# Block products for two more token tiles, and the scan's later units packed closer

## The chip, the core and the metric

The kernel runs on one core of a Trainium2 chip. Its engines each work through their own instructions in program order and wait for one another by semaphores: TensorE (PE, with its weight loads as PEld), VectorE (DVE), ScalarE (ACT), GpSimd (POOL) and SyncE (SP), which here issues DMA transfers only. The metric is device time in microseconds of one execution. The kernel before takes 340.98 us (median of 3 runs, 340.87 to 345.75).

## The reference

A gated linear-attention scan over 4 batches, 8 heads and 768 positions, in chunks, is followed by a feed-forward layer over the 3072 tokens:

```python
# per chunk: cum = cumsum(log a); L = exp(cum_i - cum_j), causal
M = (C @ B^T) * L
y = M @ x + (C @ state) * exp(cum)
state = exp(sum(log a)) * state + sum_j B_j x_j exp(cum_end - cum_j)
# then, with x = y as 3072 x 256:
h = x @ w_in            # 256 -> 2048
g = maximum(0.01 * h, h)
out = g @ w_out         # 2048 -> 256
```

Results are kept to about float32: every float32 operand of the feed-forward matmuls is split into a high and a low part, and a product is three matmuls (high x high, low x high, high x low).

## The kernel before

**The scan.** Its chunk here is 96 positions (`Q`), so there are 8 chunks of 4 batches: 32 units. A unit makes scores on PE (128-partition score banks `sc`), multiplies them on DVE with a decay tile `lt`, and then makes its outputs and the next state on PE (`unit_products`). `unit_halves` copies the state out on ACT (`stage`), from which POOL writes four small copies into the next chunk's `xs`; ACT also copies the unit's outputs, 96 tokens, into the token tiles that the feed-forward layer reads, and for most tiles DVE makes the low part `xl` right there.

Units 0 to 5 come first by themselves. Units 6 to 15 go one to each of the feed-forward steps 0 to 9 (`UNIT`), with decay made by PE. Units 16 to 31 go by pairs (`PAIR`): their decay rows are broadcast from DRAM by SP (`decay_rows`), POOL subtracts a column (`decay_sub`, L264), ACT takes the exponential and POOL selects the causal part (`decay_exp`, L272 and L273). `pair_block` (L367) makes the outputs of the last pair, the scores of the new one, the four score products on DVE (L388) and the copies. A pair stands at every fourth step from 24 to 52, and `LAST_OUT`, 56, makes the last outputs.

**The feed-forward layer.** The 3072 tokens are six tiles of 512, and the 2048 hidden features are 16 blocks of 128. A step (`ffn_in`, `ffn_act`, `ffn_low`, `ffn_out`) handles one tile and one block: six matmuls into `hp`, two activations on ACT (high part `gh`, and the activation in place), the low part `gl` on DVE, and, three steps later (`LAG`), six matmuls into two accumulator banks `op`. `CELLS` lists which tile goes with which blocks in what order: tiles 0, 1 and 2 through blocks 0 to 4, then through 5 to 15, then tile 3 through all, 64 steps. Where a cell ends, both accumulators are read out (L528 adds to an earlier part on DVE; L532 on ACT and L534 on DVE copy), before the next cell may use the banks.

Weights arrive during the first steps, 16 blocks of 512 KB. Each is decoded from 64-bit floats by ACT and by five DVE passes; `decode(n)` issues n of them at the end of a step, and `PASSES` holds n for each step.

**Tiles 4 and 5** are done last, in `two_tiles`, by Winograd's form of Strassen's algorithm for the first layer: for two blocks and two tiles it makes seven products of three matmuls where eight are usual. That takes sums of weight blocks (`sums`, `sums_split`: POOL and ACT) and sums of the two tiles (`combine`: casts and subtractions, nearly all on DVE, with two subtractions on POOL), and sums of the products out of the banks on DVE (L780, L789, L790, L796, L797). There are eight groups. In each, `slot()` gives PE output matmuls of the group before as filler. For these tiles the scan writes float32 (`x32`) and no low part. `combine` is a generator; from step `COMBINE`, 57, one piece is issued at each step.

The order of every engine is the order of the program text (`manual_schedule`); in the main loop (L818 on) a step issues: the scan's due work (`early`), `ffn_in`, `ffn_act`, `ffn_low`, a pair block if due, decode passes, a piece of `combine`, then `late` work, and last the output matmuls of step s - 3 with a cell's read-out.

Of the kernel before, what the change touches and what calls it, by code (L numbers as in the profile page):

```python
# [10 lines left out]
F32 = mybir.dt.float32  # L11
F32R = mybir.dt.float32r
# [6 lines left out]
Q = 96  # L19
NC = S // Q  # L20
QE = Q + N
# [15 lines left out]
CELLS = ((0, 0, 5), (1, 0, 5), (2, 0, 5), (0, 5, 16), (1, 5, 16), (2, 5, 16), (3, 0, 16))  # L37
TWO = (4, 5)
# [22 lines left out]
def scan_ffn(ctx: ExitStack, tc: tile.TileContext, a_l, bc_l, bn_l, x_l, w_l, out_l):  # L61
# [4 lines left out]
    px = ctx.enter_context(tc.tile_pool(name="px", bufs=4))  # L66
    pg = ctx.enter_context(tc.tile_pool(name="pg", bufs=LAG + 1))
    pob = ctx.enter_context(tc.tile_pool(name="pob", bufs=3))
# [4 lines left out]
    plt = scan.enter_context(tc.tile_pool(name="plt", bufs=4))  # L73
# [55 lines left out]
    upto_b = const.tile([Q, QE], BF16, name="upto_b")  # L129
    after = const.tile([Q, QE], F32, name="after")  # L130
    later = const.tile([Q, Q], BF16, name="later")
    less = const.tile([128, NH], BF16, name="less")
    dl = const.tile([128, SLOTS, QE], BF16, name="dl")
    dr = const.tile([128, SLOTS, NH, Q], BF16, name="dr")
    reach = [const.tile([Q, NH, Q], F32, name=f"reach{i}") for i in range(DIRECT)]
# [194 lines left out]
    def unit_halves(u, space, off=0):  # L330
# [5 lines left out]
        while i < Q:  # L336
            t, col = divmod(u * Q + i, TS)
            n = min(Q - i, TS - col)
            if col == 0 and t in TWO:
                x32[t] = mix.tile([128, 2, TS], F32, name="x32")  # L340
# [11 lines left out]
        for t, to, of in pieces:  # L352
            nc.scalar.copy((x32 if t in TWO else xh)[t][:, :, to], yp[:, :, of])
        def rest():
            for t, to, of in pieces:
                if t in TWO:
# [40 lines left out]

    w_half = [const.tile([128, NF, 2 * DM], F32R, name=n) for n in ("wh", "wl")]
# [235 lines left out]
    at(late, EARLY[-1] + 2, late_sums)  # L634
# [14 lines left out]
    def open_mix():  # L649
        nonlocal mix  # L650
        wts.close()
        mix = ctx.enter_context(tc.tile_pool(name="mix", bufs=2, side="right", reuse_waits="tile"))

    mix = bx = sp = su = None

    def open_two():
        nonlocal bx, sp, su
        scan.close()
        bx = ctx.enter_context(tc.tile_pool(name="bx", bufs=1, reuse_waits="tile"))
        sp = ctx.enter_context(tc.tile_pool(name="sp", bufs=2, reuse_waits="tile"))  # L660
# [4 lines left out]
    def sums(p):  # L665
        w32 = sp.tile([128, 2, DM], F32, name="w2")
# [17 lines left out]
    rhs = {}  # L684

    def combine():
        t1, t2 = TWO
        a, b = x32[t1], x32[t2]
        t12 = mix.tile([128, 2, TS], F32, name="t14")
        t34 = mix.tile([128, 2, TS], F32, name="t14")  # L690
        names = ("xh", "xl")
        ab = [[px.tile([128, 2, TS], F32R, name=n) for n in names] for _ in range(3)]
        ab.append([bx.tile([128, 2, TS], F32R, name=n) for n in names])
        for (h, _), x, ks in zip(ab, (a, b), (slice(0, 2), slice(1, 2))):
            nc.vector.tensor_copy(h[:, ks], x[:, ks])
        yield
# [6 lines left out]
        nc.gpsimd.tensor_tensor(  # L703
            out=ab[1][1][:, 1], in0=b[:, 1], in1=ab[1][0][:, 1], op=ALU.subtract
        )
# [7 lines left out]
        for n, (i, k) in {"11": (0, 0), "21": (0, 1), "22": (1, 1), "t1": (2, 0), "t2": (2, 1),  # L713
                          "t3": (3, 0), "t4": (3, 1)}.items():
            rhs[n] = [y[:, k] for y in ab[i]]

# [18 lines left out]
    def two_out(f, t, gh, gl, first, last):  # L735
        for m in range(2):
# [5 lines left out]
            if last:  # L742
                keep_out(t, m, outs[t][m], t == TWO[1] and m == 1)

# [7 lines left out]
    def two_tiles(queue):  # L752
        t1, t2 = TWO
        banks = score_tile()
        B, C = banks[:, 0], banks[:, 1]
        tops = score_tile()
        outs[t1] = [tops[:, m] for m in range(2)]

        def slot():
            if queue:  # L760
                queue.popleft()()

        for p in range(NP):
# [17 lines left out]
            if p + 1 < NP:  # L781
                sums(p + 1)
            slot()
            if p == 0:
                outs[t2] = [ps_o.tile([128, TS], F32, name="op") for _ in range(2)]
# [13 lines left out]
            if p + 1 < NP:  # L799
                sums_split(p + 1)  # L800
# [6 lines left out]
            order = ("11", "21", "22", "12") if p == NP - 1 else ("11", "22", "21", "12")  # L807
# [5 lines left out]
        while queue:  # L813
            slot()
# [3 lines left out]
    for s in range(total):  # L818
# [27 lines left out]
        if not passes and mix is None:  # L846
            open_mix()
        if s == COMBINE:
# [3 lines left out]
            combining = combine()  # L852
# [50 lines left out]
```

## Time and profile before

| | |
|---|---|
| median of 3 runs | 340.98 us (340.87 to 345.75) |
| profiled execution | 342.04 us, span of its instructions 340.3 us |
| PE busy | 323.8 us, 95% of the span |
| DVE, ACT, POOL busy | 201.8, 179.3, 126.1 us |
| granted TensorE clock, mean | 0.978 |
| data moved by DMA | 27.79 MB |

The profile is of one execution, and its instructions' rows give a start, an engine, the line in the kernel, the operation, and the tiles as output<-inputs. Where an engine sat idle before an instruction, brackets give how long and what ended the wait. "Groups" put together the instructions of one line and engine; "the window table" sums up busy time by engine in a stretch of the span; "the chain of waits" is followed back from the last instruction.

### The profile page before, as it was taken

The numbers are of one execution on the slowest core, as the hardware profiler recorded it, in microseconds if no ns is written. First come the engines' busy times: TensorE is split into PE (matmuls) and PEld (weight loads), VectorE is DVE, ScalarE is ACT, GpSimd is POOL, SyncE is SP. The second block draws the span as 40 slices with busy tenths as digits, with TensorE's granted clock in tenths as the row PEclk, the third lists the DMA queues.
The fourth block names the chain that finished last, engine by engine and source line by source line (L and its number), as shares of the span: only waits on it lengthen the run. The fifth ranks groups of instructions, "written<-read, shape, count | busy, mean of one in ns | idle before, by whom it ended". The sixth has DMA issues, their size and how long they took to land.

```text
span 340.3 us, 6355 instructions
## 1 busy us (share of the span) xinstructions
PE 323.8 (95%) x2410; PEld 247.7 (73%) x2412; DVE 201.8 (59%) x343; ACT 179.3 (53%) x350; POOL 126.1 (37%) x214
## 2 busy tenths in 40 slices
PE   8978899999898999999999999999999999999994
PEld 4545576778677787788888887878876787777873
DVE  5767877875787454344263243429757667556561
ACT  6555645755565654545545545343445456454551
POOL 3751413220010352733753644309224665436100
PEclk9996789999999999999999999999999999999999
DMA  7755462312783002172065121000001000000003
GB/s 223 214 190 187 153 214 65 121 57 74 219 258 113 2 1 80 64 206 93 13 174 158 44 85 64 0 2 0 0 0 64 0 0 0 2 2 0 2 0 123
DMA packets 10638, 27.79 MB, mean 82 GB/s; under 512 B 2448, under 2 KB 2544, under 8 KB 10608
## 3 DMA queue, kind: packets, MB, share of 16 engines
q1 hardware_dynamic: 9920, 24.80, 23.3%
q10 hardware_dynamic: 688, 2.59, 2.4%
q8 instruction: 19, 0.31, 0.4%
q14 instruction: 11, 0.09, 0.1%
HBM read 24.01 MB, written 3.24 MB: 80 GB/s over the span
## 4 chain that ended last, share of the span: by engine, by line
PE 81%; DVE 8%; DMA 4%; ACT 3%; issue 1%; SPq 0%; ACTq 0%
PE hp L496 26%; PE op L520 24%; PE sc L719 8%; PE sc L738 6%; PE op L738 4%; PE sc L315 3%; PE hp L719 3%; DMA raw<-w_l 2%; PE sc L298 2%; PE sc L379 2%; DMA bn<-bn_l 2%; DVE u L789 2%; DVE c L790 2%; PE sc L324 1%; PE sc L244 1%
## 5 line engine op out<-in xcount | busy, mean ns | idle before, releaser
L509 DVE TENSOR_TENSOR gl<-hp,gh 128x512 fp32r<-128x512 f32 x64 | 44.2, 691 | 79.0 <-ACT hp L506 78.0
L503 ACT ACTIVATE gh<-hp 128x512 fp32r<-128x512 f32 x64 | 38.1, 595 | 63.0 <-PE hp L496 63.0
L520 PE MATMUL op<-gh,wh 128*128 128x512 f32 x128 | 52.4, 410 | 4.0 <-DVE ob L534 2.7
L496 PE MATMUL hp<-xh,wh 128*128 128x512 f32 x128 | 52.5, 410 | 0.0
L496 PE MATMUL hp<-xh,wl 128*128 128x512 f32 x128 | 51.3, 401 | 0.0
L496 PE MATMUL hp<-xl,wh 128*128 128x512 f32 x128 | 51.1, 399 | 0.0
L351 POOL COPY xs<-stage 16x64 f32<-16x64 f32 x112 | 28.5, 255 | 60.8 <-ACT stage L348 56.5
L520 PE MATMUL op<-gh,wl 128*128 128x512 f32 x128 | 50.0, 391 | 0.0
L520 PE MATMUL op<-gl,wh 128*128 128x512 f32 x128 | 49.9, 390 | 0.0
L506 ACT ACTIVATE hp<-hp 128x512 f32<-128x512 f32 x64 | 38.0, 594 | 0.0
L520 PEld LDWEIGHTS op<-gh,wh 128*128 128x128 f32 x128 | 24.0, 188 | 12.3 <-DVE ob L534 3.5
L264 POOL TENSOR_TENSOR lt<-lt,ccol 112x768 f32<-112x768 f32 x16 | 23.5, 1471 | 23.9 <-DMA lt<-crow_d 23.3
L682 POOL TENSOR_TENSOR sl<-s,sh 128x512 fp32r<-128x512 f32 x8 | 10.4, 1295 | 56.4 <-ACT sh L681 56.4
L496 PEld LDWEIGHTS hp<-xh,wh 128*128 128x128 f32 x128 | 24.6, 192 | 7.8 <-issue 2.6
L496 PEld LDWEIGHTS hp<-xl,wh 128*128 128x128 f32 x128 | 24.9, 194 | 5.5
L496 PEld LDWEIGHTS hp<-xh,wl 128*128 128x128 f32 x128 | 24.8, 194 | 4.9
L520 PEld LDWEIGHTS op<-gl,wh 128*128 128x128 f32 x128 | 24.0, 188 | 5.2
L520 PEld LDWEIGHTS op<-gh,wl 128*128 128x128 f32 x128 | 24.1, 188 | 4.3
L273 POOL TENSOR_SCALAR_AFFINE_SELECT lt<-lt 96x768 f32<-96x768 f32 x16 | 14.0, 877 | 31.0 <-ACT lt L272 31.0
L750 DVE TENSOR_TENSOR gl<-c,gh 128x512 fp32r<-128x512 f32 x24 | 22.4, 938 | 4.8 <-PE op L738 3.1
L746 ACT ACTIVATE gh<-c 128x512 fp32r<-128x512 f32 x24 | 15.2, 632 | 18.1 <-DVE c L790 9.5
L272 ACT ACTIVATE lt<-lt 112x768 f32<-112x768 f32 x16 | 13.5, 846 | 17.4 <-POOL lt L264 17.4
(144 smaller groups left out, 604.0 us busy)
## 6 DMA issues: line engine op xcount, KB each, us to landing
raw<-w_l SPq DMA_DIRECT2D x13, 512.0 KB
lt<-crow_d SPq DMA_DIRECT2D x16, 336.0 KB
bc<-bc_l SPq DMA_DIRECT2D x7, 608.0 KB
out_l<-ob SPq DMA_DIRECT2D x12, 256.0 KB
xs<-x_l SPq DMA_DIRECT2D x7, 384.0 KB
bn<-bn_l SPq DMA_DIRECT2D x8, 231.0 KB
raw<-w_l ACTq DMA_DIRECT2D x3, 512.0 KB
bc<-bc_l ACTq DMA_DIRECT2D x1, 608.0 KB
```

Of the source, the lines that this page charges most:

```text
L264: nc.gpsimd.tensor_tensor(out=lts[u], in0=lts[u], in1=ccol[:, u * NH:(u + 1) * NH].unsqueeze(2).to_broadcast([QE, NH, Q]), op=ALU.subtract,)
L273: nc.gpsimd.affine_select(out=lt[:Q], in_=lt[:Q], pattern=[[0, NH], [1, Q]], compare_op=ALU.is_ge, fill=0.0, base=0, channel_multiplier=-1,)
L351: nc.gpsimd.tensor_copy(to[:, :, hh], stage[hh * D:hh * D + N])
L496: nc.tensor.matmul(hp, lhsT=w_half[half][:, f, k * 128:(k + 1) * 128], rhs=x[t][:, k, :], start=(n == 0), stop=(n == 5),)
L503: nc.scalar.activation(ghs[s], hp, AF.Prelu, alpha=0.01)
L506: nc.scalar.activation(hps[s], hps[s], AF.Prelu, alpha=0.01)
L509: nc.vector.tensor_tensor(out=gls[s], in0=hps.pop(s), in1=ghs[s], op=ALU.subtract)
L520: nc.tensor.matmul(op, lhsT=w_half[half][:, f, DM + m * 128:DM + (m + 1) * 128], rhs=x, start=(first and i == 0), stop=(last and i == 2),)
L719: nc.tensor.matmul(bank, lhsT=w[h], rhs=x[g], start=start and i == 0, stop=i == 2, skip_group_check=True,)
L738: nc.tensor.matmul(outs[t][m], lhsT=w_half[half][:, f, DM + m * 128:DM + (m + 1) * 128], rhs=x, start=first and i == 0, stop=last and i == 2,)
L746: nc.scalar.activation(gh, h, AF.Prelu, alpha=0.01)
L750: nc.vector.tensor_tensor(out=gl, in0=g, in1=gh, op=ALU.subtract)
```

## The change

The six cells now are tiles 0 and 1 alone, through blocks 0 to 4, 5 to 9 and 10 to 15: 32 steps. Tiles 2 to 5 get float32 from the scan, and `two_tiles` runs twice, for (2, 3) and then (4, 5): sixteen groups. The pairs of scan units stand at every second step from 12 to 26, `LAST_OUT` and `COMBINE` at 28; each unit's decay is asked for four steps ahead rather than five, and with the pairs so close a chunk's loads are issued three steps ahead of its first pair (`max(b - 12, b0 + 1)`). The late sums move from step 11 to 6. From step 10 on, `decode` gets three and two passes by turns.

The first `combine`, for tiles 2 and 3, is issued from step 28; what is left of it follows the loop. Its pieces are regrouped: the cast of tile `a` and the first two subtractions now are one piece. The second `combine`, for tiles 4 and 5, is issued inside the first `two_tiles`, a piece after each group. Between the two runs of `two_tiles` the queue of output matmuls goes on: the second's accumulators are opened by an entry of the queue. Pools change with this: `px` and `pob` have 2 buffers, a pool `pw` of 4 holds the float32 tiles, `plt` has 6 buffers, and some constants move to a pool that is closed with the scan.

```diff
-CELLS = ((0, 0, 5), (1, 0, 5), (2, 0, 5), (0, 5, 16), (1, 5, 16), (2, 5, 16), (3, 0, 16))
-TWO = (4, 5)
+CELLS = ((0, 0, 5), (1, 0, 5), (0, 5, 10), (1, 5, 10), (0, 10, 16), (1, 10, 16))
+TWOS = ((2, 3), (4, 5))
...
-PAIR = {16: 24, 18: 28, 20: 32, 22: 36, 24: 40, 26: 44, 28: 48, 30: 52}
-LAST_OUT = 56
-COMBINE = 57
-
-PASSES = (5, 5, 5, 3, 3, 3, 3, 2, 3, 3) + (3,) * 12
+PAIR = {16: 12, 18: 14, 20: 16, 22: 18, 24: 20, 26: 22, 28: 24, 30: 26}
+LAST_OUT = 28
+COMBINE = 28
+SUMS_AT = 6
+
+PASSES = (5, 5, 5, 3, 3, 3, 3, 2, 3, 3) + (3, 2) * 8
...
-            at(early, b - 5 + e, decay_rows, u + e)
+            at(early, b - 4 + e, decay_rows, u + e)
             at(early, b - 3 + e, decay_sub, u + e)
             at(early, b - 2 + e, decay_exp, u + e)
...
-    def combine():
...
-        for (h, _), x, ks in zip(ab, (a, b), (slice(0, 2), slice(1, 2))):
-            nc.vector.tensor_copy(h[:, ks], x[:, ks])
-        yield
+    def combine(pair, pools, temps, rhs):
...
+        nc.vector.tensor_copy(ab[0][0], a)
         nc.vector.tensor_tensor(out=t12[:, 0], in0=b[:, 0], in1=a[:, 0], op=ALU.subtract)
         nc.vector.tensor_tensor(out=t34[:, 0], in0=b[:, 1], in1=b[:, 0], op=ALU.subtract)
         nc.gpsimd.tensor_tensor(out=ab[0][1], in0=a, in1=ab[0][0], op=ALU.subtract)
         yield
         nc.vector.tensor_tensor(out=t12[:, 1], in0=b[:, 1], in1=t12[:, 0], op=ALU.subtract)
         nc.vector.tensor_tensor(out=t34[:, 1], in0=a[:, 1], in1=t12[:, 1], op=ALU.subtract)
...
+        nc.vector.tensor_copy(ab[1][0], b[:, 1])
+        nc.gpsimd.tensor_tensor(out=ab[1][1], in0=b[:, 1], in1=ab[1][0], op=ALU.subtract)
         yield
...
+    def two_tiles(queue, pair, rhs, after_group):
...
+        def opens():
+            open_outs(t1, t2)
+
+        queue.append(opens)
...
-        while queue:
-            slot()
+            after_group(p)
...
-    two_tiles(collections.deque(
-        [lambda s=s: ffn_out(s) for s in range(total - LAG, total)]
-    ))
+    for _ in combining:
+        pass
+    queue = collections.deque([lambda s=s: ffn_out(s) for s in range(total - LAG, total)])
+    temps = [pw.tile([128, 2, TS], F32, name="x32") for _ in range(2)]
+    combining = combine(TWOS[1], (px, by, px, by), temps, rhs_of[1])
+    two_tiles(queue, TWOS[0], rhs_of[0], lambda p: next(combining, None))
+    two_tiles(queue, TWOS[1], rhs_of[1], lambda p: None)
+    while queue:
+        queue.popleft()()
```

More of the change, by code (lines that the diff above doesn't have):

```diff
@@ L741, in two_out @@
                 )
-            if last:
-                keep_out(t, m, outs[t][m], t == TWO[1] and m == 1)
+        if last:
+            for m in range(2):
+                keep_out(t, m, outs[t][m], t == NT - 1 and m == 1)
     def act_split(h, gh, in_place):
@@ L780, in two_tiles @@
             nc.vector.tensor_tensor(out=u2, in0=B, in1=kept, op=ALU.add)
-            if p + 1 < NP:
-                sums(p + 1)
+            if p + 1 < NP or t2 < NT - 1:
+                sums((p + 1) % NP)
             slot()
-            if p == 0:
-                outs[t2] = [ps_o.tile([128, TS], F32, name="op") for _ in range(2)]
             product(A, False, a12, rhs["21"])
@@ L851, in scan_ffn @@
             sums_split(0)
-            combining = combine()
+            with_temps = [su.tile([128, 2, TS], F32, name=n) for n in ("t12", "t34")]
+            rhs_of = [{}, {}]
+            combining = combine(TWOS[0], (bx,) * 4, with_temps, rhs_of[0])
         if combining:
```

88 lines of the change are left out of this document (44 added, 44 removed).

## The prediction

> **What bounds the kernel now.** I read the page first, then the chain of waits, then three stretches of the window table, then the timeline around every gap of the matmul engine. The page says that one engine is the program:
>
> ```profile
> span 340.3 us, 6355 instructions
> ...
> PE 323.8 (95%) x2410; PEld 247.7 (73%) x2412; DVE 201.8 (59%) x343; ACT 179.3 (53%) x350; POOL 126.1 (37%) x214
> ...
> PE 81%; DVE 8%; DMA 4%; ACT 3%; issue 1%; SPq 0%; ACTq 0%
> ```
>
> PE is busy for 95% of the span and carries 81% of the chain that ended last. So an edit pays only where it takes matmuls away, and costs wherever PE is made to wait. Three prices of PE work follow, from the chain of waits around 150 us (start, length, work) and the window table (the stretch, its length, then busy time of PE, PEld, DVE, ACT, POOL, granted clock, DMA share, GB/s):
>
> ```profile
> 151.31 1.36 PE hp L496 x6
> 152.67 1.36 PE op L520 x6
> ```
>
> ```profile
> 148.43:161.44 13.01, 13.01 (x129) 10.56 (x128) 5.34 (x11) 6.67 (x15) 6.54 (x12) 1.00 0.52 161
> 293.55:304.23 10.68, 10.53 (x45) 8.36 (x45) 6.78 (x10) 5.87 (x10) 5.43 (x6) 1.00 0.00 2
> ```
>
> A step of twelve matmuls takes 1.36 + 1.36 = 2.72 us, 0.227 us a matmul. The first stretch is four steps and one pair of scan units: 13.01 - 4 x 2.72 = 2.13 us of PE for a pair. The second stretch is one group of seven block products, 45 matmuls in 10.68 us, where four plain steps (48 matmuls) would take 10.88.
>
> **The exchange itself.** Tiles 2 and 3 leave 32 steps and become eight groups. By count that is 8 x 3 = 24 matmuls fewer, 24 x 0.227 = 5.4 us. But a group does not run at the matmul rate: 45 x 0.227 = 10.2, so 0.46 us of it is a wait, and the timeline shows which:
>
> ```profile
> 282.15 0.69 DVE L790 TENSOR_TENSOR c<-sc,u 128x512 f32<-128x512 f32 x1
> ...
> 282.36 0.39 PE L738 MATMUL op<-gl,wh 128*128 128x512 f32 x1
> 282.90 0.50 PE L719 MATMUL sc<-xh,wh 128*128 128x512 f32 x1
> ```
>
> The bank sums on DVE end at 282.84 and the next product starts behind them; PE's last filler, issued at 282.36, had its 0.23 us by 282.6. The new groups have the same order, so I price them alike: 32 x 2.72 - 8 x 10.68 = 87.0 - 85.4 = **1.6 us saved**. The scan's matmuls are the same in number, so packing the pairs changes PE's work by nothing; it changes what the other engines must do in the time.
>
> **Cell boundaries.** Where a cell ends, the accumulators in `op` must be read out before the next cell's first output matmul. PE's gaps at such places, and DVE's order at the first of them:
>
> ```profile
> 87.60 0.50 PE L520 MATMUL op<-gh,wh 128*128 128x512 f32 x1 [1.09 <-DVE ob L534]
> 103.14 0.50 PE L520 MATMUL op<-gh,wh 128*128 128x512 f32 x1 [1.61 <-DVE ob L534]
> 207.99 0.47 PE L520 MATMUL op<-gh,wh 128*128 128x512 f32 x1 [0.54 <-DVE ob L528]
> ```
>
> ```profile
> 84.94 0.68 DVE L443 TENSOR_TENSOR wl<-w,wh 128x512 fp32r<-128x512 f32 x1
> ...
> 86.86 0.68 DVE L534 COPY ob<-op 128x512 f32<-128x512 f32 x1
> ```
>
> Together 1.09 + 1.61 + 0.54 = 3.2 us now. DVE works in program order: three decode passes (84.94 to 86.86, 1.92 us) stand ahead of the read-out, and PE waits for it. In the new order the boundaries fall behind steps 12, 17, 22 and 28. Rows for what is put in between:
>
> ```profile
> 146.15 0.86 PE sc L379 x16
> ...
> 223.74 0.80 PE sc L315 x32
> ```
>
> ```profile
> 147.08 1.95 DVE L388 TENSOR_TENSOR lt<-sc,lt 112x384 f32<-112x384 f32 x4
> ```
>
> Step 12 (first pair): DVE gets four score products more, PE 0.86 us of scores: 1.09 + 1.95 - 0.86 = 2.2. Step 17: the following step has a pair, whose 2.13 us of PE cover it: 0. Step 22: 1.09 + 1.95 - 2.13, and 0.68 more because both read-outs are now DVE additions, so the first three matmuls wait, not the last three: 1.6. Step 28 is worse: its three decode passes are gone, but `COMBINE` now stands at 28, and the first piece of `combine` is issued ahead of that step's read-outs. Its instructions ran once in this trace:
>
> ```profile
> 231.20 2.52 POOL L699 TENSOR_TENSOR xl<-x,xh 128x1024 fp32r<-128x1024 f32 x1 [0.63 <-DVE xh L695]
> ```
>
> ```profile
> 232.03 2.23 DVE L697 TENSOR_TENSOR t<-x,x 128x512 f32<-128x512 f32 x1
> 234.19 1.78 DVE L698 TENSOR_TENSOR t<-x 128x512 f32<-128x512 f32 x1
> ...
> 239.06 1.64 DVE L708 CAST xh<-t 128x1024 fp32r<-128x1024 f32 x2
> 241.22 1.21 DVE L710 TENSOR_TENSOR xl<-t,xh 128x1024 fp32r<-128x1024 f32 x1
> ```
>
> A cast of a whole tile is 1.64 / 2 = 0.82; the two subtractions took 2.23 and 1.78 while POOL worked on the same kind of operands, and the L443 row, with POOL idle, prices the like at 0.68. So the piece costs 0.82 + 0.68 x 2 = 2.2 to 0.82 + 2.23 + 1.78 = 4.8. POOL's 2.52 us begin after the cast and cover the first subtraction and little of the second: 0.82 + 2.23 + 0.8 = 3.85, the value I take. The wait is 1.09 + 0.68 - 1.92 + 3.85 - 0.80 (last products on PE) = 2.9, between 1.2 and 3.9. Sum 2.2 + 0 + 1.6 + 2.9 = 6.7 against 3.2: **3.5 us lost** (1.8 to 4.5). The rest of the first `combine` (2 x 0.82 + 2 x 1.21 and the short pieces) ends about when PE reaches the first group, delayed itself by 2.9; it costs nothing more unless that delay is absent, when it costs about the same.
>
> [...]
>
> **The second combine, inside the groups.** Its pieces stand on DVE behind a group's last low part and ahead of the next group's first bank sum, `u2`, which PE needs before it may add to that bank. What that place is worth now:
>
> ```profile
> 257.73 0.68 DVE L534 COPY ob<-op 128x512 f32<-128x512 f32 x1
> ...
> 259.06 0.50 PE L719 MATMUL sc<-xh,sh 128*128 128x512 f32 x1 [0.46 <-DVE u L780]
> ```
>
> ```profile
> 278.76 0.69 DVE L780 TENSOR_TENSOR u<-sc,kept 128x512 f32<-128x512 f32 x1 [0.21 <-PE sc L719]
> ...
> 280.55 0.39 PE L719 MATMUL sc<-xh,sh 128*128 128x512 f32 x1
> ```
>
> After the first group one copy of 0.68 already makes PE wait 0.46: there is no slack there. Now two additions and the first piece stand in that place. Here POOL goes on from its subtraction to the next group's sums, so I take both subtractions near their contended price: 0.6 + 4.8, less 0.7 because the three low parts ahead of them run while POOL waits for the cast: **4.7 us more** (0.6 + 2.2 = 2.8 to 5.4). After the later groups the slack is 280.55 - 278.76 - 0.69 = 1.1, and the pieces are about 1.6, 1.64, 1.21 and 1.21: 0.5 + 0.5 + 0.1 + 0.1 = 1.2 (0 to 3). Before the last eight groups the read-out is no longer in the way: -0.5. Sum **5.4 us lost**.
>
> **The scan by twos.** A pair now has two steps and its own work, 2 x 2.72 + 2.13 = 7.57 us, for what it had 13.01 us before:
>
> ```profile
> 148.19 0.21 ACT L348 COPY stage<-sc 128x64 f32<-128x64 f32 x1 [1.92 <-DVE lt L388]
> ...
> 149.24 0.33 ACT L353 CAST xh<-sc 128x192 fp32r<-128x192 f32 x1
> ```
>
> ```profile
> 143.36 1.06 POOL L279 TENSOR_TENSOR bn<-bn,erev 112x512 f32<-112x512 f32 x1
> 148.54 2.16 POOL L351 COPY xs<-stage 16x64 f32<-16x64 f32 x8 [4.12 <-ACT stage L348]
> 150.78 1.47 POOL L264 TENSOR_TENSOR lt<-lt,ccol 112x768 f32<-112x768 f32 x1
> 153.21 0.88 POOL L273 TENSOR_SCALAR_AFFINE_SELECT lt<-lt 96x768 f32<-96x768 f32 x1 [0.95 <-ACT lt L272]
> ```
>
> ```profile
> L503 ACT ACTIVATE gh<-hp 128x512 fp32r<-128x512 f32 x64 | 38.1, 595 | 63.0 <-PE hp L496 63.0
> ```
>
> POOL per pair: 2 x 1.47 + 2 x 0.88 + 2.16 + 1.06 / 2 = 7.4 us, nearly all of it. And POOL is in a circle: its subtraction releases ACT's exponential (0.95 with its wait), ACT's two activations come next in order (2 x 0.6), then DVE's low part (0.69), two score products (1.11 from 147.08 to 148.19), the stage copy and the way to POOL (0.35), eight copies (2.16), a select (0.88) and the next subtraction (1.47): 8.8 us round, 1.2 more than 7.57. It turns six times, until the last chunk writes no state: 7.4 us of lag. Against it stand the slack to the next pair's score banks (read until 149.24 + 0.33 = 149.57; the pair's work on PE began 2.13 - 0.86 us ahead of its scores, at 144.9, so the next one's would at 144.9 + 7.57 = 152.5: 2.9) and PE's own pauses at steps 12 and 22 (3.8), in which the circle catches up: 6.7. I take 0 net, between 0 and 7.4. DVE itself has 1.95 + 2 x 0.69 + five decode passes (5 x 0.64 = 3.2) = 6.5 of 7.57, enough if POOL does not slow the passes. The SP queue issues row broadcasts, chunk loads and the last weight loads in a closer order; the stretch from 148.43 holds two broadcasts and a whole chunk load at a DMA share of 0.52 of 13.01 us, so even all of it in 7.57 us would be 0.89: bandwidth does not bind, though a broadcast may land late by some tenths behind a weight load, which the circle's bounds take in. The late sums move from step 11 to 6 with the same matmuls: 0, 0.5 at most for their banks. No low part of x for units 11 to 15: 0 to -0.5.
>
> **Sum.** -1.6 + 3.5 + 5.4 + 0 = +7.3 us. The profiled execution took 342.04 us, 340.3 of span and 1.74 around it; it becomes 349.3. The median of the runs shown, 340.98, is 1.06 below that execution, so I forecast **348.3 us**. What a measurement here can tell from no change is about 2%, 6.8 us: 334.2 to 347.8. The forecast lies just outside.
>
> **Rivals.** *The additions hide* (not slower): subtractions run at 0.68, the later pieces fit, the circle has slack. Then boundaries cost 1.8, the second combine 2.8 - 0.5 = 2.3: -1.6 + 4.1, **343.5**; were the waits mostly gone as well, 339. For it: DVE is only 59% busy and each group leaves it idle at several places. Against: the order is fixed and the 0.46 us row shows a place without slack.
>
> *The circle binds* (slower still): if POOL's chain gives no lag back, 7.4 - 2.9 = 4.5 us come on top, more if POOL's company also slows the decode passes: **353 to 356**. It decides once the circle is longer than 7.57 us; the 1.92 wait of the stage copy speaks for it, PE's pauses against.
>
> *The clock drops.* Granted clock is the third column from the end:
>
> ```profile
> 28.50:38.70 10.20, 9.92 (x60) 6.20 (x58) 8.09 (x16) 4.71 (x10) 1.75 (x2) 0.50 0.70 229
> ...
> 339.20:340.30 1.10, 0.00 (x0) 0.00 (x0) 0.00 (x0) 0.00 (x0) 0.00 (x0) 0.50 0.00 0
> ```
>
> Half speed was granted for 10.20 us in the first stage and again at the end, after PE had stopped. A pause of 5 us inside the groups may do the same; a stretch of 3.4 us, a third of the row above, at half speed costs 1.7 us, two such 3.4: **350 to 352**. The longest pause after 80 us is 1.61 and drew no drop, so the trace leaves it open. [...]
>
> *Faster by over 2%*: all boundary waits vanish too and the groups lose their 0.46: 340.98 - 5.4 - 3.2 = 332.4. Nothing in the trace supports that.
>
> **Chances.** Forecast 0.42, additions hidden 0.30, circle 0.16, clock 0.10, faster 0.02. Half of the forecast's own spread (345 to 351) lies within 2%: same 0.30 + 0.19 = 0.49, slower 0.23 + 0.16 + 0.10 = 0.49, faster 0.02. The range takes the hidden case in to 339.5 and the circle up to 355.
>
> **What would show it.** PE gaps released by `ob` near steps 12, 22 and 28, the last the longest; one PE gap of about 5 us released by `u` in the second of sixteen groups; groups of 10.68 from the sixth on. POOL near 95% between the pairs, ACT's exponential waiting for it. If the gap in the second group is under 2 us, or the pairs take over 8 us each, my sum is wrong in that term.

## The result, and the profile after

The changed kernel takes 372.21 us (median of 4 runs, 368.31 to 373.51) against 340.93 us for the kernel before beside it (4 runs): a ratio of 1.092, 95% interval 1.081 to 1.103. It is slower, as forecast, but by 31 us and not by 7; the time lies outside the range of 339.5 to 355. Ratios and their intervals here are of the runs near each kernel's fastest alone, so they can differ from the quotient of two medians. The profiled execution took 372.13 us. From its page:

```profile
span 370.4 us, 6422 instructions
...
PE 329.4 (89%) x2388; PEld 247.3 (67%) x2388; DVE 245.0 (66%) x383; ACT 191.2 (52%) x366; POOL 187.8 (51%) x264
...
PE 59%; DVE 18%; ACT 6%; POOL 5%; DMA 5%; issue 4%; SPq 2%; ACTq 0%; DVEq 0%; POOLq 0%
```

PE's share of the chain fell from 81% to 59%, and its busy time rose by 5.6 us although it has 22 instructions fewer: a first sign of a lower clock (granted 0.949 on the mean, 0.978 before). To see where the 30.1 us of span went, I divided both executions where a step or a group issues its first matmul into `hp`:

| stretch | before, us | after, us | more |
|---|---|---|---|
| start to step 10 | 75.25 | 77.27 | 2.0 |
| step 10 to the first group | 169.78 (54 steps) | 102.68 (22 steps) | 19.9, when the 32 steps that are gone count 32 x 2.72 = 87.0 |
| groups to the end | 95.27 (8) | 190.45 (16) | 8.1 more than those 87.0 for the eight more groups |

The first is no effect of the change to speak of: kernels that are alike up to step 10 reach it at 73.5 to 80.1 us. The second holds most of the loss. The window table for the 18 steps of the scan by twos (step 10 to step 28), with columns as in the prediction:

```profile
77.27:166.73 89.46, 72.47 (x762) 55.94 (x761) 54.41 (x90) 45.24 (x96) 64.15 (x86) 0.89 0.41 120
```

At the prediction's own prices PE needs 18 x 2.72 + 8 x 2.13 = 66.0 us there; it took 89.5. No engine is full: DVE is busy for 61% of it, POOL for 72%. So this looks like a circle of waits rather than a bound by one engine's load. The circle can be timed where it passes DVE. From the first score product of a pair to that of the next (a turn, in what follows) it takes 10.79, 10.91, 10.89, 10.94, 10.91 and 11.61 us, and the last time, with the decoding over and no subtraction left on POOL, 7.43. The first turn has no state copies yet. The five behind it take 55.3 us, where two steps and a pair on PE need 5 x 7.57 = 37.9: 17.4 us, most of the loss of 23.5 in these steps. The timeline of PE shows where the lag is paid (start, length, last the idle time in front and what ended it):

```profile
93.38 0.80 PE L524 MATMUL op<-gh,wh 128*128 128x512 f32 x1 [4.66 <-DVE ob L538]
...
117.52 0.50 PE L524 MATMUL op<-gh,wh 128*128 128x512 f32 x1 [2.39 <-DVE ob L532]
...
132.92 0.50 PE L500 MATMUL hp<-xh,wh 128*128 128x512 f32 x1 [1.80 <-DVE gl L513]
...
147.82 0.79 PE L524 MATMUL op<-gh,wh 128*128 128x512 f32 x1 [7.99 <-DVE ob L532]
...
172.98 0.50 PE L524 MATMUL op<-gh,wh 128*128 128x512 f32 x1 [0.99 <-DVE ob L532]
...
183.03 0.50 PE L716 MATMUL sc<-xl,sh 128*128 128x512 f32 x1 [1.78 <-DVE xl L706]
...
201.48 0.79 PE L716 MATMUL sc<-xh,sh 128*128 128x512 f32 x1 [4.31 <-DVE u L789]
```

Four are read-outs at the ends of cells (93.38, 117.52, 147.82, 172.98). What DVE has been held up by gathers until PE must wait for DVE, and that is there. Matmuls of 0.79 and 0.80 us behind a pause are longer than the 0.50 of the others, and the window table says why (granted clock third from the end):

```profile
91.70:98.50 6.80, 5.12 (x45) 3.83 (x49) 3.24 (x6) 1.66 (x3) 3.84 (x3) 0.50 0.86 271
119.00:122.40 3.40, 3.40 (x9) 2.64 (x8) 1.17 (x3) 2.35 (x4) 2.45 (x3) 0.51 0.01 3
142.90:153.10 10.20, 5.28 (x12) 3.79 (x12) 8.83 (x13) 4.72 (x11) 8.13 (x13) 0.50 0.00 1
183.90:187.30 3.40, 3.40 (x10) 2.66 (x9) 1.17 (x2) 0.00 (x0) 0.79 (x1) 0.50 0.00 0
201.00:204.40 3.40, 2.92 (x7) 2.34 (x8) 1.63 (x3) 0.00 (x0) 2.70 (x5) 0.50 0.02 5
```

Half speed was granted beside each pause but those of 0.99 us and, at 132.92, of 1.80, for 27.2 us in all; in the kernel before no such stretch lies between 80 and 339 us. What PE worked in these stretches (20.1 us busy) would have taken about half that at full speed (six output matmuls took 2.56 us at 184.40, and 1.36 at 152.67 in the kernel before), so the drops cost up to 10 us, less where PE had to wait anyway. Of the three in the scan, the second costs the circle nothing, as the turns beside it (10.89 and 10.94 us) are like their neighbours at full speed, and the turn around the third is 0.7 us longer than these. The first (5.12 us busy) may cost up to 2.6 us, the two in the groups (3.40 and 2.92) up to 3.2 together.

Why did a pause of 1.78 us draw half speed and one of 1.80 not? The shortest stretches of half speed in this trace lasted 3.4 us. I compared windows of that length, two that end where the clock fell (119.04 and 183.90 us) and one that ends four such lengths behind the first of them:

| window, us | PE busy, us | pause in it | granted behind it |
|---|---|---|---|
| 115.63 to 119.04 | 1.52 of 3.41 (45%) | 2.39 | half speed |
| 180.48 to 183.90 | 1.64 of 3.42 (48%) | 1.78 | half speed |
| 129.28 to 132.70 | 1.84 of 3.42 (54%) | most of 1.80 | full speed |

Behind the two with less PE work the clock fell. But 1.66 us of it from 364.80 to 368.22 were followed by full speed, and in the kernel before 2.61 us from 38.73 to 42.14, beside the single scan units, by half. So the length of a pause alone did not decide it in this trace; what did is not shown.

**Who holds up whom.** The timeline of POOL and DVE over a pair of the changed kernel:

```profile
121.23 0.69 DVE L513 TENSOR_TENSOR gl<-hp,gh 128x512 fp32r<-128x512 f32 x1 [3.17 <-ACT hp L510]
...
123.31 4.60 POOL L354 COPY xs<-stage 16x64 f32<-16x64 f32 x8 [0.69 <-ACT stage L351]
...
132.11 1.47 POOL L267 TENSOR_TENSOR lt<-lt,ccol 112x768 f32<-112x768 f32 x1
132.17 0.69 DVE L513 TENSOR_TENSOR gl<-hp,gh 128x512 fp32r<-128x512 f32 x1 [4.36 <-ACT hp L510]
132.78 1.94 DVE L391 TENSOR_TENSOR lt<-sc,lt 112x384 f32<-112x384 f32 x4
...
134.25 2.11 POOL L354 COPY xs<-stage 16x64 f32<-16x64 f32 x1 [0.67 <-ACT stage L351]
134.64 0.42 DVE L420 TENSOR_SCALAR w<-w 128x512 uint32<-128x512 uint32 x1
134.97 0.68 DVE L447 TENSOR_TENSOR wl<-w,wh 128x512 fp32r<-128x512 f32 x1
135.57 0.68 DVE L427 SCALAR_TENSOR_TENSOR w<-raw,w 128x512 uint32<-128x512 uint32 x1
```

The eight copies that took 2.16 us in the kernel before take 4.60. A single one, of 16 x 64 elements, lasts 2.11 us: it begins before three decode passes that DVE runs back to back and ends at 136.36, when the last of them has ended (135.57 + 0.68 = 136.25). The other way round, earlier in the same trace:

```profile
83.23 1.47 POOL L267 TENSOR_TENSOR lt<-lt,ccol 112x768 f32<-112x768 f32 x1
83.53 2.74 DVE L434 SCALAR_TENSOR_TENSOR w<-raw,w 128x512 uint32<-128x512 uint32 x1
84.66 1.06 POOL L282 TENSOR_TENSOR bn<-bn,erev 112x512 f32<-112x512 f32 x1
...
85.68 1.33 POOL L276 TENSOR_SCALAR_AFFINE_SELECT lt<-lt 96x768 f32<-96x768 f32 x1
86.19 2.54 DVE L414 TENSOR_SCALAR w<-w 128x512 f32<-128x512 f32 x1
86.98 1.47 POOL L267 TENSOR_TENSOR lt<-lt,ccol 112x768 f32<-112x768 f32 x1
```

A pass of 0.68 us lasts 2.74 under two POOL instructions, one of 0.42 lasts 2.54. In the kernel before POOL did little from step 10 until the decoding was over (the row below: 10.85 us of 54.28), and the pairs' state copies came after it; the change lays the two side by side. The window row of the kernel before, from its step 10 on:

```profile
75.25:129.53 54.28, 51.58 (x239) 41.74 (x238) 34.28 (x59) 31.81 (x59) 10.85 (x12) 1.00 0.37 112
```

In these rows a DVE pass lasts over more than one POOL instruction in a row (83.53 to 86.27 us, over those at 83.23 and 84.66), and a copy over three passes. What makes the two engines hold each other up is not shown by the rows.

### The profile page after: what moved, and what is told of

Read it like the earlier page. It is cut to its first block, busy times and chain, and to the rows that moved or that the text cites. A ratio compares the mean times of both kernels' runs of the same rounds, so it can differ in the third digit from the quotient of the medians.

```text
span 370.4 us, 6422 instructions
## 1 busy us (share of the span) xinstructions
PE 329.4 (89%) x2388; PEld 247.3 (67%) x2388; DVE 245.0 (66%) x383; ACT 191.2 (52%) x366; POOL 187.8 (51%) x264
## 4 chain that ended last, share of the span: by engine, by line
PE 59%; DVE 18%; ACT 6%; POOL 5%; DMA 5%; issue 4%; SPq 2%; ACTq 0%; DVEq 0%; POOLq 0%
PE sc L716 16%; PE sc L735 11%; PE hp L500 8%; PE op L735 7%; PE op L524 7%; PE hp L716 5%; DVE u L796 3%; DVE c L797 3%; DVE lt L391 2%; DMA bc<-bc_l 2%; POOL xs L354 2%; POOL lt L267 2%; DMA bn<-bn_l 2%; PE sc L318 2%; PE sc L301 2%
## 5 line engine op out<-in xcount | busy, mean ns | idle before, releaser
L513 DVE TENSOR_TENSOR gl<-hp,gh 128x512 fp32r<-128x512 f32 x32 | 22.1, 689 | 39.7 <-ACT hp L510 37.2
L524 PE MATMUL op<-gh,wh 128*128 128x512 f32 x64 | 28.9, 452 | 16.0 <-DVE ob L532 11.4
L745 ACT ACTIVATE c<-c 128x512 f32<-128x512 f32 x48 | 30.4, 632 | 1.5
L716 PE MATMUL sc<-xh,sh 128*128 128x512 f32 x64 | 25.8, 403 | 4.9 <-DVE u L789 4.8
L500 PE MATMUL hp<-xh,wh 128*128 128x512 f32 x64 | 28.5, 445 | 1.8 <-DVE gl L513 1.8
L500 PE MATMUL hp<-xh,wl 128*128 128x512 f32 x64 | 27.4, 428 | 0.0
L500 PE MATMUL hp<-xl,wh 128*128 128x512 f32 x64 | 27.4, 428 | 0.0
L716 PE MATMUL sc<-xl,sh 128*128 128x512 f32 x64 | 25.5, 398 | 1.8 <-DVE xl L706 1.8
L668 POOL TENSOR_TENSOR w<-wh,wl 128x512 f32<-128x512 f32 x16 | 27.0, 1689 | 0.0
L524 PE MATMUL op<-gl,wh 128*128 128x512 f32 x64 | 26.2, 410 | 0.0
L735 PE MATMUL sc<-gh,wh 128*128 128x512 f32 x64 | 25.1, 392 | 0.6 <-DVE ob L729 0.6
```

The source lines that it names most:

```text
L500: nc.tensor.matmul(hp, lhsT=w_half[half][:, f, k * 128:(k + 1) * 128], rhs=x[t][:, k, :], start=(n == 0), stop=(n == 5),)
L513: nc.vector.tensor_tensor(out=gls[s], in0=hps.pop(s), in1=ghs[s], op=ALU.subtract)
L524: nc.tensor.matmul(op, lhsT=w_half[half][:, f, DM + m * 128:DM + (m + 1) * 128], rhs=x, start=(first and i == 0), stop=(last and i == 2),)
L668: nc.gpsimd.tensor_tensor(out=w32, in0=wh[:, 2 * p:2 * p + 2, :DM], in1=wl[:, 2 * p:2 * p + 2, :DM], op=ALU.add,)
L716: nc.tensor.matmul(bank, lhsT=w[h], rhs=x[g], start=start and i == 0, stop=i == 2, skip_group_check=True,)
L735: nc.tensor.matmul(outs[t][m], lhsT=w_half[half][:, f, DM + m * 128:DM + (m + 1) * 128], rhs=x, start=first and i == 0, stop=last and i == 2,)
```

## The experiments

The kernel before on the same chip took 343.79 us (one run) beside runs 1 to 4, 341.53 us (13 runs) beside 5, 6, 9 and 13, 343.07 us (7 runs) beside 8, 10 and 11, and 341.9 us (7 runs) beside 7 and 12. Runs 1 to 9 are single runs, and the four of the changed kernel spread over 5.2 us, so a few us of a whole time say little there. "18 steps" is the stretch from step 10 to step 28 of the profiled execution; it is steadier: 89.5, 89.7 and 89.0 us in the three kernels that are alike up to there (the changed one, runs 1 and 9). "A turn" is the mean of the second to the fifth.

**1. Tiles 2 and 3 by plain steps again**

```diff
-CELLS = (..., (0, 10, 16), (1, 10, 16))
+CELLS = (..., (0, 10, 16), (1, 10, 16), (2, 0, 16), (3, 0, 16))
```

> The first 32 steps of the changed kernel, with the scan by twos, but tiles 2 and 3 then go through 32 plain steps and only tiles 4 and 5 through block products. If the scan by twos is what costs (the circle POOL - ACT - DVE at about 10.9 us a pair instead of 7.57): the first 32 steps end at 180 us as in the changed kernel, then 32 x 2.72 = 87 and 95 us as before: 362 us, between 357 and 367. If the second run of block products and its combine are what costs: 341 to 347.

(The parts of tiles 2 and 3 are made by DVE from the float32 tiles at steps 28 and 29.) 359.93 us; 18 steps 89.7, the same as in the changed kernel (89.5). So some 24 us over PE's own 66.0 are there without a single new group: the scan by twos alone. (The whole is 16 us above the kernel before: the 3.2 us of that one's pauses at cell ends are not in the 66.0, and the rest is within what single runs tell.) From step 28 to the end it took 195.0 us, the changed kernel 203.7: the second run of block products costs 8.7 us instead of saving 1.6.

**2. Four of five decode passes left out for blocks 9 to 15**

```diff
 def decode_hold(f):    # likewise decode_shift, decode_sign, decode_low
+    if f >= 9:
+        return
```

> The changed kernel, with four of the five DVE decode passes left out for weight blocks 9 to 15 (so those blocks hold other numbers). If POOL's eight copies are held up by the passes on DVE (2.1 us for a copy that takes 0.25 alone): the copies fall from 4.6 to 2.2 to 2.8 us a pair, a pair takes 8.8 to 9.3 us, the pause at step 13 goes too: 350 to 360 us. If the circle is long by itself and the passes play no part: pairs stay above 10.5 us, 367 us or more.

360.4 us, 0.4 above the theory's bound, with step 10 reached 2.8 us later than in the changed kernel; 18 steps 76.2, 13.3 less. The eight copies took 2.5 to 2.8 us instead of 4.2 (sums of the rows alone; 1.87 in the kernel before). A turn fell from 10.91 to 9.50 us, by as much as the copies, though not to the 8.8 to 9.3 expected. So DVE's passes are one piece of the circle and not the whole of it: without them it is still longer than 7.57.

**3. The copies by DVE, straight from PSUM**

```diff
-nc.gpsimd.tensor_copy(to[:, :, hh], stage[hh * D:hh * D + N])
+nc.vector.tensor_copy(to[:, :, hh], space[hh * D:hh * D + N, :, off + Q:off + Q + D])
```

> The changed kernel, with the eight state copies of a pair made by DVE from the score banks instead of ACT's stage copy and POOL. If the copies behind the passes are the long link: a pair's circle goes through ACT's second exponential and POOL's select, 0.95 + 1.2 + 0.69 + 1.95 + 0.66 + 0.95 + 0.88 + 1.47 = 8.75 us: 354 to 363 us. If POOL's other work is held up by the passes as much: 366 us or more.

376.8 us, 18 steps 91.9: the rival's range. With the copies gone from POOL, its other instructions hold up DVE, on which the copies now stand:

```profile
128.83 1.46 POOL L267 TENSOR_TENSOR lt<-lt,ccol 112x768 f32<-112x768 f32 x1
129.29 2.57 DVE L440 SCALAR_TENSOR_TENSOR w<-raw,w 128x512 uint32<-128x512 uint32 x1
130.26 1.05 POOL L282 TENSOR_TENSOR bn<-bn,erev 112x512 f32<-112x512 f32 x1
```

**4. POOL's subtraction ahead of its select in the same step**

```diff
-            at(early, b - 2 + e, decay_exp, u + e)
+    for u, b in PAIR.items():        # after all decay_sub
+        for e in range(2):
+            at(early, b - 2 + e, decay_exp, u + e)
```

> The changed kernel, with POOL's subtraction issued ahead of the select of the same step, so that the next subtraction waits for no exponential. If POOL's load with the held-up copies (2 x 1.47 + 2 x 0.88 + 4.6 + 0.5 = 9.8 us a pair) is what binds: pairs take 9.8 to 10.4 us, 365 to 370 us. If it is the ring of waits, which this cuts: pairs near 7.6 to 8.5 us, 352 to 360 us.

369.06 us, 18 steps 83.4, a turn 10.08 us: both in the ranges given for POOL's load (365 to 370 us, pairs of 9.8 to 10.4). POOL's order was worth 0.83 us a turn; in its place POOL itself is nearly full, busy for 18.37 of the 20.18 us of two turns from 109.81.

**5. The copies by ACT, straight from PSUM**

```diff
-nc.gpsimd.tensor_copy(to[:, :, hh], stage[hh * D:hh * D + N])
+nc.scalar.copy(to[:, :, hh], space[hh * D:hh * D + N, :, off + Q:off + Q + D])
```

> The changed kernel, but the eight copies of a pair's state go from PSUM to xs on ACT, with no stage tile and no copy on POOL (the early units keep POOL's). Theory (POOL's copies, held up to 4.6 us a pair beside DVE's decode passes, are the largest piece of the circle): POOL's select no longer stands behind them, POOL has 5.2 us a pair, ACT about 6.5 of 7.57; the 18 steps from step 10 to step 28 go from 89.5 us to 66 to 76, the whole from 372 to 350 to 360. Rival (the circle only moves, as it did when DVE made the copies: ACT's activations now come late): 85 us or more for the 18 steps, 366 us or more.

372.3 us, 18 steps 86.7: the rival. POOL's busy time in the stretch fell to 42.24 us of 86.65, and still only 2.8 us of it were won: the exponential, in ACT's order behind copies that wait for DVE, comes late. Waits between 105 and 122 us (total, times, longest):

```profile
POOL lt L276 <- ACT lt L275: 12.3, 2, 7.3
```

**6. No passes, and the subtraction first**

> The changed kernel without four of the five DVE decode passes of the weight blocks 9 to 15 (their weights are then not the decoded ones: this part of the computation is left out) and with both of POOL's subtractions of a step ahead of its selects. Each alone took 13.3 and 6 us off the 18 steps from 10 to 28. Theory (two separate pieces of one circle, hold-ups beside DVE and the order on POOL): they add up, 89.5 us become 68 to 73, near the 65 of PE's own work, and the time is 350 to 356. Rival (one and the same piece): 75 us or more, 357 or more.

358.17 us, 18 steps 73.2: the time is 2 us above the theory's bound and in the rival's range (357 or more), with step 10 reached 2.1 us later than in the changed kernel, and the steps are just above the theory's 73. The turn decides it: 8.69 us, 2.22 less than in the changed kernel, where run 2 took 1.41 off and run 4 0.83. They add up. The window row of the 18 steps:

```profile
79.36:152.55 73.19, 67.88 (x762) 53.12 (x760) 36.52 (x63) 45.49 (x96) 55.90 (x85) 0.95 0.51 147
```

Steps 16 to 22 (99.74 to 122.46 us by the first matmul of a step) take 22.72 us, 7.57 a pair, the figure of the prediction for PE alone. But that is PE using up its lead: the circle still turns 1.12 us slower, and one pause of 4.8 us was left at the end of the third cell, about what four such turns add up to.

**7. Memsets in place of these passes**

```diff
 def decode_hold(f):    # likewise the other three
+    if f >= 9:
+        nc.vector.memset(w32, 1.0)
+        return
```

> The changed kernel with POOL's subtractions ahead of its selects, and for the weight blocks 9 to 15 each of four decode passes replaced by a memset of the same tile on DVE, so that DVE is about as busy but reads nothing from SBUF there (the decoding of these blocks is left out). Theory (what costs is that DVE and POOL hold each other up while both read SBUF, not DVE's load): POOL's eight copies of a pair stay near 2.5 us and the 18 steps from 10 to 28 near the 73.2 us of the run with no passes, 71 to 76, the time 355 to 361. Rival (DVE's load, 6.5 of the 7.57 us of a pair, and its order): 79 us or more for the 18 steps, 364 or more.

360.63 us, 18 steps 77.1, the copies of a pair 2.7 to 2.8 us: between the two, nearer to the theory, though above its 76. The rows of the groups and of the window:

```profile
L354 POOL COPY xs<-stage 16x64 f32<-16x64 f32 x112 | 32.9, 294 | 45.3 <-ACT stage L351 34.3 <-issue 6.3
...
L434 DVE MEMSET w<- 128x512 f32 x7 | 3.4, 485 | 0.4
```

```profile
79.64:156.71 77.07, 68.67 (x761) 53.64 (x760) 50.51 (x90) 45.31 (x96) 56.30 (x85) 0.93 0.48 140
```

DVE is busy for 50.5 us, against 54.3 in run 4, which has the same order and the real passes, and the stretch is 6.3 us shorter; against run 6 it has 14 us of DVE work more and is 3.9 us longer. The turns tell where:

| kernel | copies of a pair, us | first turn | a turn | 18 steps |
|---|---|---|---|---|
| changed | 4.2 | 10.79 | 10.91 | 89.5 |
| run 4, subtraction first | 4.0 to 4.2 | 9.86 | 10.08 | 83.4 |
| run 2, four of five passes left out | 2.5 to 2.8 | 7.51 | 9.50 | 76.2 |
| run 6, as run 2, subtraction first | 2.6 to 2.8 | 7.53 | 8.69 | 73.2 |
| run 7, memsets, subtraction first | 2.7 to 2.8 | 11.16 | 8.72 | 77.1 |

In runs 6 and 7 a turn is the same within 0.03 us, so DVE's load costs the circle nothing, and the 1.36 us a turn between runs 4 and 7 is what the copies are shorter. That raw buffers come free earlier when no pass reads them leaves no mark there. The 3.9 us between runs 6 and 7 lie in the first turn, which has no copies: in run 7 the read-out behind step 12 has two memsets and a pass that was held to 1.75 us ahead of it, PE pauses for 2.62 us there instead of 0.53, and the clock granted over the 18 steps is 0.93 instead of 0.95.

**8. The output matmuls ahead of the pair's work**

```diff
 if s in pair_at:
+    ffn_out(s - LAG)
     pair_block(*pair_at[s])
```

> The changed kernel with the output matmuls and read-outs of a step that has a pair issued ahead of the pair's work instead of behind it. Theory (the circle sets the rate and the 8 us gap at the boundary behind step 22 is only the place where its lag is paid): the gap goes, but the pairs' matmuls wait for their score banks instead, and the 18 steps from 10 to 28 still take 84 us or more, the whole 366 to 374. Rival (the boundary itself costs: read-outs on DVE stood behind multiplications that wait for POOL, and elsewhere the lag is covered): 75 us or less for the 18 steps, 358 or less.

370.59 us, 18 steps 86.0. The first turn fell from 10.79 to 7.70 us, but the five with copies took 57.7 instead of 55.3, with the pauses at other places. For these the boundary is the place where the lag is paid, not its source; the read-out behind step 12 did cost for itself. (The long gap did not go, as I had expected: it fell to about 5 us, and another of about 5 stood at 115 us.)

**9. The second combine cut finer, behind the read-outs**

```diff
+        if pair == TWOS[1]:
+            yield                  # ahead of each of the first two subtractions
...
-        if combining:              # now after ffn_out(s - LAG)
-            next(combining, None)
```

> The changed kernel with the read-outs of the scan's steps ahead of the pieces of combine, and the first piece of the second combine cut in three over as many groups. Theory (the 4.3 us gap in the second group, and the half-clock stretch beside it, come from that piece standing ahead of the group's first bank sum): the gap falls under 1 us, no half clock near it, and the time from step 28 to the end goes from 203.7 to 196 to 200. Rival (the gap is that of POOL's sums of the weights, or the pieces only wait at another place): 202 or more from step 28 to the end.

365.15 us; step 28 to the end 200.3 us instead of 203.7, just above the theory's 200. The gap in the second group went from 4.31 to 1.07, just above its 1, with no half clock near it. The pause of 0.99 at the end of the fourth cell is gone too, but the first combine's now is longer, with half clock beside it still:

```profile
180.34 0.80 PE L720 MATMUL sc<-xl,sh 128*128 128x512 f32 x1 [2.81 <-DVE xl L710]
...
195.43 0.50 PE L720 MATMUL sc<-xh,sh 128*128 128x512 f32 x1 [1.07 <-DVE u L793]
```

**10. Four repairs at once** (runs 4, 5, 9, and the group order of run 13)

> The changed kernel with four repairs at once: the pair's state copies on ACT out of PSUM, both POOL subtractions of a step ahead of its selects, read-outs ahead of the pieces of combine with the second combine's first piece cut in three, and in each group the product of s3 ahead of that of a12. Theory (copies on ACT alone gained 3 us of the 18 steps from 10 to 28 only because the exponential, behind the copies in ACT's order, then held the next subtraction; with the subtractions ahead, that circle opens too): the 18 steps take 68 to 76 us instead of 89.5, step 28 to the end 196 to 200, the time 345 to 355, ratio to before 1.01 to 1.04. Rival (the hold-ups between POOL and DVE are enough to keep a pair at 9 us or more): 80 us or more for the 18 steps, 358 or more.

359.87 us (4 runs, 355.61 to 364.02; the stretches are of the execution of 362.93), ratio 1.039 (1.031 to 1.047); 18 steps 84.0, step 28 to the end 197.4. The rival for the scan, the theory for the groups; the whole is in the rival's range by its median and at the end of the theory's (1.01 to 1.04) by its ratio. Waits from 100 to 128 us:

```profile
POOL lt L267 <- DMA lt<-crow_d: 12.1, 3, 4.8
```

POOL now waits for the row broadcasts, and these stand on SP's queue, on which the raw load ahead waits for a decode pass (from 85 to 150 us):

```profile
SPq L92 <- DVE w L440: 23.6, 3, 9.9
SPq L262 <- PE sc L318: 13.5, 5, 5.6
```

**11. The same, and the output matmuls first**

> The four repairs together, and the output matmuls and read-outs ahead of the pair's work. Theory (with the circle open there is little lag left to pay, so the order of the read-outs is worth only what stands ahead of them at the four boundaries, 2 to 4 us): 342 to 351. Rival (the boundaries cost for themselves): 336 to 341, as the kernel before or below it.

365.94 us (4 runs), ratio 1.068 (1.059 to 1.076): neither. Putting the read-outs first made the mended kernel worse; why is not known.

**12. The four repairs, and the raw load behind the broadcasts on SP**

```diff
 def do_low(f):
-    fetch_w(f + RAWS)
+    fetches.append(f + RAWS)      # issued in the next step, behind `early`
```

> The four repairs together, and the load of the next raw weight block issued on the SP queue a step later, behind the row broadcasts. Theory (in the run of the four repairs POOL waited 12 us for three broadcasts because they stood behind a raw load that waits for a late decode pass): these waits fall under 4 us, the 18 steps go from 84 to 72 to 78 us, the time to 346 to 353. Rival (the broadcasts wait for their own buffers, or the passes stay late and the wait goes to them): 81 us or more, 356 to 362.

359.95 us (4 runs, 358.29 to 364.55; the stretches are of the execution of 364.55), ratio 1.049 (1.041 to 1.058); 18 steps 85.8: the rival. From 79 to 165 us POOL's waits put down to broadcasts fell from 14.8 to 9.0 us, but SP's waits before it can issue a broadcast into an `lt` buffer grew from 24.8 to 33.8 us (85 to 150 us). So the order on this queue was worth some of that wait and no time: what is late on it waits for passes and pairs that are late themselves.

**13. The kernel before, with one exchange in the group**

```diff
+            product(B, False, s3, rhs["t3"])
             product(A, False, a12, rhs["21"])
             act_split(A, g["11"][0], A)
-            product(B, False, s3, rhs["t3"])
```

> The kernel before with one exchange: in each group the product of s3 into bank B is issued ahead of the product of a12 into bank A, so that it lies over the DVE sum that the next product into C waits for. Theory (the 0.46 us by which a group of 10.68 exceeds its 45 matmuls are that wait): 8 x 0.46 = 3.7 us less, 336.5 to 338.5. Rival (the wait goes to the next link, the sum behind bank A, now issued later): 339.5 to 343.

339.94 us (10 runs) against 341.53 (13 runs), ratio 0.995 (0.989 to 1.000): not to be told from no change, though the mechanism is there. The middle groups take 10.20 us each, with PE busy throughout; 9.75 us of one of them:

```profile
287.31:297.06 9.75, 9.75 (x45) 8.07 (x44) 7.03 (x9) 5.48 (x10) 4.97 (x7) 1.00 0.01 2
```

Over the eight groups to the end it is 92.2 us instead of 95.3, 3.1 less where 3.7 were expected; the rest of the profiled execution was 1.4 us longer up to the groups.

## Why the prediction was wrong

**The step that failed** is "The scan by twos", in "I take 0 net". Its circle was the right one: POOL's subtraction, ACT's exponential, the activations, the low part, the score products, the copies, the select. The chain of waits of the changed kernel runs through just these links, and DVE's low part returns at 121.23 and again at 132.17 us, 10.9 us round, where I had 8.8 and a pair of steps needs 7.57. Of the six turns that I counted, five have copies, and these lost 17.4 us where the term had 7.4 at most and took 0. Two things were wrong with it.

- *A price taken where the neighbour was idle.* The 2.16 us of the copies came from a row at 148.54 us of the kernel before, when DVE had no decode passes left. Beside them it is 4.60: 8.8 + 2.44 = 11.2, within 0.3 of what was measured. Run 2 shows the cause: with four of the five passes gone the copies and the turn both fell by about 1.4 us. I had used the hold-up between POOL and DVE for the subtractions of `combine`, and named it for the passes only as a rival's extra, but did not put it on the copies.
- *Slack counted that is none.* I let PE's pauses at steps 12 and 22 (3.8 us) pay for the lag. A pause at a boundary is the lag, arriving; it hides nothing. No turn was shortened by one, and in run 8, with the pauses at other places, the five turns took no less. Even at the 8.8 us of my sum the lag would have been 7.4 us with only the 2.9 of the score banks against it.

**The rivals.** *The circle binds* is what happened, but five turns lost 17.4 us where this rival had 7.4, or 4.5 with the banks' slack. Its point of decision, a circle longer than 7.57 us, was right, and so was its remark that POOL's company may slow the passes. *The clock drops* happened as well, and not only in the groups: five stretches. One stood beside a pause of 2.39 us, one beside 1.78, though a pause of 1.80 (at 132.92) drew none. So it was not the length of the pause alone; PE was busy for 1.52, 1.64 and 1.84 us of the 3.4 in the windows shown with these three.

**The exchange** (-1.6): right for undisturbed groups; late in the changed kernel they start 10.65 to 10.69 us apart. **Cell boundaries** (2.2, 0, 1.6, 2.9): measured 4.66, 2.39, 7.99 and 0.99. The first comes after two passes that POOL held to 2.74 and 2.54 us, 4.2 more than they take alone, and its pause is 0.53 in run 6, without these passes; the next two hold the circle's lag. Step 17 was covered only if the pair came on time. At step 28 PE did wait for the first piece of `combine`, as the DVE rows show:

```profile
170.07 0.78 DVE L693 CAST xh<-x 128x1024 fp32r<-128x1024 f32 x1
170.78 0.94 DVE L694 TENSOR_TENSOR t<-x,x 128x512 f32<-128x512 f32 x1
171.64 0.68 DVE L695 TENSOR_TENSOR t<-x 128x512 f32<-128x512 f32 x1
172.25 1.28 DVE L532 TENSOR_TENSOR ob<-op,ob 128x512 f32<-128x512 f32 x2
```

The read-outs stand right behind the piece, but it ran near its lower price, 2.2 us, as POOL was still at the sums of the weights and began its own subtraction only at 173.42. So the wait is just under my lower bound of 1.2. **The first combine** I had ended "about when PE reaches the first group", delayed by 2.9, and had said that without this delay it costs about the same there. So it did: PE waited 1.78 us for it, 0.99 + 1.78 = 2.77 in all, and in run 9, without the 0.99, 2.81. **The second combine**: 4.7 more predicted after the first group; the pause is 4.31 where the kernel before has 0.46, 3.85 more, as only one of the two subtractions was held up (2.83 us, the other took 0.69). Run 9 shows that its first piece is the cause. That the groups lost 8.1 us and not 3.8 is the 1.78, which my sum has at step 28, and up to 3.2 us of half speed, less the 0.85 that the second combine came out lower: 7.9 together. **The SP queue**: bandwidth does not bind, as written (DMA share 0.41 over the 18 steps), but a queue that waits for passes and pairs is late with them; "some tenths" became 12 us of waits in run 10.

**What stays open.** No version of the scan beside the real decode passes came below 83 us for the 18 steps in its profiled execution. Of the 3.3 us by which a turn exceeds 7.57, the hold-up of the copies is 1.4 and POOL's order 0.8; the last 1.1 no run removed, and with both repaired the copies still took 2.6 to 2.8 us, against 1.87 in the kernel before. How much of the first turn is the clock, and what in runs 10 to 12 took the place of POOL's copies, was not taken apart. Nor was one version run in which the pairs wait until the decoding is over and tiles 2 and 3 still go by products. None beats the kernel before by more than can be measured.

## What to carry to other kernels

In these traces a duration was a property of an instruction and of its company. Before a row's price is carried to another place, look at what the other engines do there: here the price of POOL's copies doubled, from 2.16 to 4.60 us a pair, because DVE's passes ran beside them, and a copy of 0.27 us lasted 2.11 beside a run of three passes, not the 0.68 of one.

When in-order queues form a circle longer than the loop it feeds (10.91 us against 7.57 here), only its length counts: pauses elsewhere are where the lag shows, and taking one link off one engine moved the wait to the next queue (DVE, ACT, SP in runs 3, 5 and 10). Add up the circle with contended prices and compare it with the period before counting any slack; and time a repair by the turn, where pieces add up (1.41 and 0.83 apart, 2.22 together), rather than by steps, which mix it with the places where the lag is paid.

## What the runs showed of the hardware

- POOL and DVE held each other up for whole runs of instructions: a POOL copy, 2.16 / 8 = 0.27 us in the kernel before, lasted 2.11 to 2.14 us in the changed kernel beside three DVE passes, DVE passes of 0.68 and 0.42 lasted 2.74 and 2.54 us under POOL's. Two cases of DVE operations with one input from PSUM showed no such hold-up: the four products at 132.78 took 1.94 us, as in the kernel before, with POOL's subtraction beside the first of them, and POOL's copies at 67.58 us, beside the low part L513 (67.70, 0.69 us), 0.23 to 0.24 us each. DVE memsets in run 7 left the copies at 2.7 to 2.8 us a pair, as in run 6, where these passes are left out without memsets in their place (2.6 to 2.8).
- From 80 us until PE had finished, half speed was granted in the changed kernel in five stretches, of 6.8, 3.4, 10.2, 3.4 and 3.4 us, beside pauses of PE of 4.66, 2.39, 7.99, 1.78 and 4.31 us; pauses of 0.99 and 1.80 us had none beside them. It followed 1.52 and 1.64 us of PE in a window of 3.4 us, and did not follow 1.84 in one or 1.66 in another.
